# Attention before two expert layers on one core: the short tile's sums by GpSimd, the next batch's sums in parts, values read earlier

## The chip, the cores and the metric

The kernel runs on one core of a Trainium2 chip. Times are microseconds of device time for one execution; single stretches and instructions are given in the same unit, from the start of the profiled span.

## The reference

Attention over 4 batches, 8 heads, 576 tokens and 64 dimensions, in float32, with a bias from running sums, and then two layers of the kind x, activation, x on the 2304 tokens (512 to 2048 to 512).

```
scores = scale * q @ k^T                       # [4, 8, 576, 576], causal
cum    = cumsum(maximum(s, 0), -1)             # [4, 8, 576]
scores = scores + minimum(-(cum[:, None] - cum[None, :]), 0)
attn   = softmax(scores);  x = attn @ v        # [2304, 512] after joining the heads
h = x @ w_in;   x = (h * tanh(softplus(h))) @ w_out
h = x @ w2_in;  out = (h * sigmoid(1.702 h)) @ w2_out
```

The bias of a row is the same constant for every column except for the column's own running sum, so the kernel only adds the sum of the column and lets the row's extreme value take out the rest.

## The kernel before

**Tiling.** Per batch there are five tiles of query rows, four of 128 and a short one of 64 (576 = 4 x 128 + 64). The 8 heads come in two groups of 4. A group of one tile is worked off in steps: each step does the scores of one or several heads (`do_qk`, on TensorE), adds the running sums and takes the extreme value in one VectorE instruction (`do_max`, line 525, in the trace the custom instruction that reads `s` and `ck`), exponentials on ScalarE (`do_exp`), a split in two float16 parts (`do_hilo`, line 550), which are brought to the layout of the second product by a transposing DMA on SP (`pt<-hl`), and four steps later the product with v (`do_av`). In the short tile two heads share the 128 partitions: heads 0 and 1 of a group stand in partitions 0 to 63, heads 2 and 3 in 64 to 127. Batch 0 is done in another form that transposes on TensorE; there the running sums of its first two tiles come through a product.

**The running sums in SBUF.** They are computed once, written to DRAM (`cum_d`), and read back broadcast over the partitions. `load_ck` (line 372) allocates a tile of 128 x (4 heads x 512 columns) for one group, and loads it in two parts, columns 0 to 127 and 128 to 511. There is one buffer for each group (tag `ck0`, `ck1`). `load_ckp` (line 384) is for the short tile: it allocates a new tile in the same buffer, named `cp` in the trace, so that it waits for the last reader of `ck`, and loads 64 partitions x 2 heads x 576 columns twice, with DMAs on SP. The call stands after the last step of the fourth tile's group (line 695); the call for the next batch's sums stands after the last step of the short tile's group (line 697).

**The values' scale.** The split of v needs the largest value of the batch. `vscale_load` (line 310) reads all of a batch's v in three loads of 384 KB on SP into three rotating buffers (`vl`, of the five in pool `mo_a`, which the first layer's results `hs` use as well) and takes three maxima on VectorE (`vm`); `vscale_set` (line 321) makes the scale. `VSTEP` (line 639) says with which tile and group of the batch before they are queued: both with the short tile, group 0 and group 1. Steps of preparation are queued two groups ahead (`queue_prep(gi + 2)`, line 682), and popped over the steps of the group that runs, so the loads come out with the fourth tile's scores.

**Order.** The code is one emission order; a planner then orders each engine's instructions by readiness, with this order as priority. Each engine and DMA queue takes its instructions in order. SP issues the transposing DMAs, the sums, the values for the scale and the first layer's results `h_d`; GpSimd issues the loads of k, q and v (`kraw`, `qraw`, `vraw`), splits some weights and normalises x. The first layer's products (`h<-xh,w`) run on TensorE between the attention's from the first tiles on, up to about 410 us; the rest of the layers follows.

At the start some products without use keep TensorE busy while the first loads come (`warm`, line 813); they are the same in both kernels.

Of the kernel before, what the change touches and what calls it, by code (L numbers as in the profile page):

```python
# [9 lines left out]
F32 = mybir.dt.float32  # L10
# [79 lines left out]
def attention_moe_moe_kernel(  # L90
# [12 lines left out]
    nc = Line(tc.nc, lambda i, j: tc.add_manual_dep(i, j.name, order, reason="order of emission"))  # L103
    B, H, S, D = q.shape
# [6 lines left out]
    HG = H // 2  # L111
# [10 lines left out]
    cum_d = dram.tile([B, H, S], F32, name="cum_d")  # L122
# [18 lines left out]
    ck_p = enter(tc.tile_pool(name="ck", bufs=1))  # L141
# [36 lines left out]
    def held(d):  # L178
        if anchor[0] is not None and nxt[0] < NEAR:
            tc.add_manual_dep(d.ins, anchor[0].ins.name, order, reason="not before these scores")  # L180
        return d
# [153 lines left out]
    LK = S // 128 * 128  # L335
# [34 lines left out]
    ck, ckp = {}, {}  # L370

    def load_ck(b, g):
        t = ck_p.tile([128, HG * LK], F32, tag=f"ck{g}", name=f"ck{g}").rearrange("p (h t) -> p h t", t=LK)
        ck[b, g] = t
        load_ck_part(b, g, 0, 128)
        load_ck_part(b, g, 128, LK)

    def load_ck_part(b, g, c0, c1):
        held(nc.sync.dma_start(
            out=ck[b, g][:, :, c0:c1],  # L380
            in_=cum_d[b:b + 1, g * HG:(g + 1) * HG, c0:c1].to_broadcast([128, HG, c1 - c0]),
        ))

    def load_ckp(b, g):
        t = ck_p.tile([128, HG * LK], F32, tag=f"ck{g}", name=f"cp{g}")
        t = t[:, 0:HG // 2 * S].rearrange("p (h t) -> p h t", t=S)
        for a in range(2):
            h0 = g * HG + 2 * a
            nc.sync.dma_start(
                out=t[64 * a:64 * a + 64], in_=cum_d[b:b + 1, h0:h0 + 2, :].to_broadcast([64, 2, S])  # L390
            )
        ckp[b, g] = t

# [18 lines left out]
    last_of = {}  # L412
    for idx, x in enumerate(steps):
        gi = groups.index((x["b"], x["i"], x["g"]))
# [89 lines left out]
    def do_qk(x):  # L504
        b, i, g, n, L = x["b"], x["i"], x["g"], x["n"], x["L"]
        x["S"] = []
        for c0, c1 in segs(x):
            ps = ps_s.tile([128, 512], F32, tag="s", name="s")
            x["S"].append(ps)
            for e, hs in enumerate(x["hs"]):  # L510
                o = ps[:, e * L:e * L + c1 - c0]
                for a, h in enumerate(hs):
                    hl = h - g * HG
                    for w in range(2):
                        nc.tensor.matmul(
                            out=o, lhsT=qw[b, i, g][:, hl, w, :], rhs=kw[b, g][:, hl, c0:c1],
                            start=(e == a == w == 0), stop=False, skip_group_check=True,
                        )
                if c1 == L:
                    anchor[0] = nc.tensor.matmul(  # L520
                        out=o[:, c1 - c0 - n:c1 - c0], lhsT=identb, rhs=maskb if n == 128 else maskp,
                        start=False, stop=True, skip_group_check=True,
                    )

    def do_max(x):
        b, i, g, L = x["b"], x["i"], x["g"], x["L"]
        mx = sm_p.tile([128, HG], F32, tag="mx", name="mx")
        x["P"] = p = pp.tile([128, S], F32, tag="P", name="P", bufs=PB)
        for e, hs in enumerate(x["hs"]):
            hl = hs[0] - g * HG  # L530
            c = ckp[b, g][:, hl] if len(hs) == 2 else ck[b, g][:, hl]
            for f, (c0, c1) in enumerate(segs(x)):
                nc.vector.tensor_tensor_reduce(
                    out=p[:, e * L + c0:e * L + c1], in0=x["S"][f][:, e * L:e * L + c1 - c0], in1=c[:, c0:c1],
                    scale=1.0, scalar=mx[:, e:e + 1] if f else 3.0e38, op0=ALU.add, op1=ALU.min,
                    accum_out=mx[:, e:e + 1],
                )
        x["mx"] = mx

    def do_exp(x):  # L540
        ts = tile_state(x)
        L, p = x["L"], x["P"]
        for e in range(x["mu"]):
            o = p[:, e * L:(e + 1) * L]
            lut(
                o, o, AF.Exp, bias=x["mx"][:, e:e + 1], scale=-1.0,
                accum_out=ts["sums"][:, x["j"] + e, 0:1],
            )

    def do_hilo(x):  # L550
        L, mu, nb = x["L"], x["mu"], x["nb"]
        w = mu * L
        nblk = 2 * w // 128
        hl = pp.tile([128, 2 * NTIL * 128], F16, tag="hl", name="hl", bufs=HLB)
        p = x["P"]
        nc.scalar.activation(out=hl[:, 0:w], in_=p[:, 0:w], func=AF.Copy, scale=PSC)
        body = w // 128 * 128
        for c0, c1, o in ((0, body, 2 * w - body), (body, w, w)):
            if c0 < c1:
                nc.vector.scalar_tensor_tensor(  # L560
                    out=hl[:, o:o + c1 - c0], in0=p[:, c0:c1], scalar=PSC, in1=hl[:, c0:c1],
                    op0=ALU.mult, op1=ALU.subtract,
                )
        x["T"] = d = pt_p.tile([128, 2 * NTIL, 128], F16, tag="pt", name="pt")
        last_pt[0] = nc.sync.dma_start_transpose(out=d[:, 0:nblk, :], in_=hl[:, 0:2 * w])
# [70 lines left out]
    prep_q = []  # L636
    late_k = {}

    VSTEP = {(4, 0): vscale_load, (4, 1): vscale_set}

    NE = 4

    def queue_prep(gi):
        if gi >= len(groups):
            return
        b, i, g = groups[gi]
        items, vs, kT = split_items(b, i, g)
        if b == 0 and i == 2:
            for i_ in range(2):
                prep_q.append(lambda i_=i_: k_turn(0, i_, g, raw.pop((0, i_, g))))  # L650
        if NE < gi < len(groups) - 1:
            prep_q.append(lambda: load_group(*groups[gi + 1]))
        if i == 0 and b > 0:
            late_k[groups.index((b - 1, NTIL - 1, g))] = kT
        else:
            items = items + [kT]
        items = items + vs
        if b + 1 < B and (i, g) in VSTEP:
            items = items + [lambda: VSTEP[i, g](b + 1)]
        prep_q.extend(items)  # L660

    def pop_prep(m):
        for _ in range(min(m, len(prep_q))):
            prep_q.pop(0)()
# [8 lines left out]
    def tick():  # L673
        t = nxt[0]
        nxt[0] += 1
        if t < NS:
            x = steps[t]
            gi = x["gi"]
            if first_of[gi] == t:
                if gi > NE:  # L680
                    pop_prep(len(prep_q))
                queue_prep(gi + 2)
            if t >= NEAR:
                nc.mode = None
            left = last_of[gi] - t + 1
            npop = -(-len(prep_q) // left)
        else:
            npop = len(prep_q)
        if t < NS:
            do_qk(x)  # L690
            do_max(x)
            do_exp(x)
            if last_of[gi] == t and gi in late_k:
                late_k.pop(gi)()
            if last_of[gi] == t and x["i"] == LK // 128 - 1:
                load_ckp(x["b"], x["g"])
            if last_of[gi] == t and x["i"] == NTIL - 1 and x["b"] + 1 < B:
                load_ck(x["b"] + 1, x["g"])
            if x["b"]:
                do_hilo(x)  # L700
        pop_prep(npop)
        if 0 < t <= NS and steps[t - 1]["b"] == 0:
            early_pt(steps[t - 1])
        while avn[0] < NS and t - avn[0] >= lag(avn[0])[0]:
            x = steps[avn[0]]
            if x["b"]:
                do_av(x)
            else:
                early_av(x)
            if x["last"]:  # L710
                if x["b"]:
                    norm_tile(x)
                emit_q.append((t + lag(avn[0])[1], x))
            avn[0] += 1
        while emit_q and emit_q[0][0] <= t:
            emit_tile(emit_q.pop(0)[1])
# [110 lines left out]
    for t in q0:  # L827
# [4 lines left out]
        out=maskb, in_=maskb, pattern=[[-1, 128]], compare_op=ALU.is_ge, fill=BIG, base=0, channel_multiplier=1  # L832
# [62 lines left out]
    for a in range(2):  # L895
        nc.gpsimd.affine_select(
            out=maskp[64 * a:64 * a + 64], in_=maskp[64 * a:64 * a + 64], pattern=[[-1, 64]],
# [114 lines left out]
    while attn_left():  # L1012
        tick()
# [13 lines left out]
    for m in range(NF):  # L1027
        if m % 2 == 0:
            t = tmp_pair(F32, "hs")
        o = t[:, m % 2 * 512:m % 2 * 512 + 512]  # L1030
# [4 lines left out]
        if m % 2:  # L1035
            nc.sync.dma_start(
                out=h_d[:, m - 1:m + 1, (NU - UE) * U:NT], in_=t.rearrange("p (m t) -> p m t", m=2)
# [193 lines left out]
    for i, (u, t0, W, m0, n) in enumerate(groups1):  # L1231
# [10 lines left out]
        for j in range(n):  # L1242
# [3 lines left out]
            for c in range(KC):  # L1246
                a, o = divmod(c * W, 512)
# [125 lines left out]
    for u, (s0, W) in enumerate(spans):  # L1373
        for t0 in range(0, W, U):
            for jp in range(NP // 2):
# [10 lines left out]
                for e in range(2):  # L1386
                    o = slice(e * 512, (e + 1) * 512)
# [40 lines left out]
```

## Time and profile before

| what | us or share |
| --- | --- |
| median of 3 runs | 1015.3 (1012.83 to 1019.54) |
| profiled execution, its own time | 1021.99 |
| span in the profile | 1020.2 |
| TensorE busy | 973.8 |
| VectorE busy | 672.6 |
| ScalarE busy | 553.6 |
| GpSimd busy | 264.3 |
| mean granted clock | 0.99 |

The profile is that of one execution. All instructions that go through the kernel's recording helper have the same line (L76), so groups are read by the names of the tiles: `out<-in`.

### The profile page before, as it was taken

How to read it: one execution, taken by the hardware profiler on the slowest of the kernel's cores; microseconds unless marked ns; L12 is line 12 of the kernel's file. 1: busy time of each engine (PE TensorE's matmuls, PEld its weight loads, DVE VectorE, ACT ScalarE, POOL GpSimd, SP SyncE). 2: the span in 40 equal slices, each digit the busy share in tenths (PEclk: the TensorE clock that was granted, in tenths of full speed). 3: DMA queues.
4: the chain of work that ended last, by engine and by line, in shares of the span. 5: the costliest groups of instructions: out<-in, count | busy, mean ns of one | idle time of the engine just before them, and what ended most of it. 6: DMA issues, size and time to landing. Idle time of an engine off the chain costs nothing.

```text
span 1020.2 us, 20171 instructions
## 1 busy us (share of the span) xinstructions
PE 973.8 (95%) x7974; PEld 866.2 (85%) x7974; DVE 672.6 (66%) x1363; ACT 553.6 (54%) x1062; POOL 264.3 (26%) x318
## 2 busy tenths in 40 slices
PE   8889999968989999999999999999999999999997
PEld 7778988858979878998888888988888888888886
DVE  6679777754566787587998994994654653653553
ACT  4666677655646876486655663753433433433331
POOL 4634431233112410000000000054424434243341
PEclk9999999998999999999999999999999999999999
DMA  9932678996599969799997653400100100000000
GB/s 260 308 105 78 195 163 210 207 166 157 122 187 211 201 140 185 247 337 365 380 322 248 206 200 118 158 2 1 63 22 1 42 22 1 22 22 2 21 17 27
DMA packets 154863, 146.46 MB, mean 144 GB/s; under 512 B 89904, under 2 KB 123184, under 8 KB 154768
## 3 DMA queue, kind: packets, MB, share of 16 engines
q1 hardware_dynamic: 148352, 126.94, 45.4%
q0 software_dynamic: 6416, 18.23, 7.7%
q8 instruction: 63, 1.03, 0.4%
q14 instruction: 32, 0.26, 0.1%
HBM read 93.28 MB, written 32.58 MB: 123 GB/s over the span
## 4 chain that ended last, share of the span: by engine, by line
PE 81%; DMA 9%; DVE 5%; issue 2%; ACT 1%; POOL 1%; SPq 0%; DVEq 0%; POOLq 0%; ACTq 0%
PE h L76 29%; PE acc L76 24%; PE p L76 16%; DMA pt<-hl 5%; PE s L76 5%; PE o L76 3%; DMA kraw<-in_k_dram 2%; PE kt L76 1%; DVE wst L76 1%; PE qt L76 1%; PE pt L76 1%; PE xt L76 1%; DMA qraw<-in_q_dram 1%; POOL w L76 1%; DMA vl<-in_v_dram 0%
## 5 line engine op out<-in xcount | busy, mean ns | idle before, releaser
L76 PE MATMUL h<-x,w2i 128*128 128x256 f16 x1728 | 199.9, 273 | 0.9 <-DVE z L76 0.9
L76 PE MATMUL h<-xh,w 128*128 128x256 f32 x1344 | 193.4, 292 | 3.4 <-POOL w L76 3.2
L76 PEld LDWEIGHTS <-w2i 128*128 128x128 f16 x1728 | 169.0, 98 | 20.7 <-issue 1.1
L76 PE MATMUL acc<-gh,w 128*128 128x512 f32 (+1 forms) x640 | 181.7, 369 | 0.0
L76 PEld LDWEIGHTS h<-xh,w 128*128 128x128 f32 x1344 | 170.9, 193 | 6.0 <-POOL w L76 4.0
L76 PE MATMUL p<-w2l,gh 128*128 128x256 f16 x504 | 136.0, 273 | 0.0
L76 PE MATMUL p<-w2h,gl 128*128 128x256 f16 x504 | 135.9, 273 | 0.0
L76 PEld LDWEIGHTS acc<-gh,w 128*128 128x128 f32 x640 | 116.1, 189 | 20.6
L76 PE MATMUL p<-w2h,gh 128*128 128x256 f16 x504 | 133.3, 273 | 0.2 <-DVE e L76 0.2
L76 PE MATMUL acc<-gl,w 128*128 128x512 f32 (+1 forms) x320 | 117.9, 368 | 0.0
L76 DVE TENSOR_TENSOR gl<-z,gh 128x1024 fp32r<-128x1024 f32 (+1 forms) x72 | 94.5, 1313 | 27.9 <-ACT gh L76 27.0
L76 POOL TENSOR_TENSOR s<-z 128x256 f32<-128x256 f32 x72 | 56.4, 803 | 214.7 <-DVE z L76 214.7
L76 PEld LDWEIGHTS <-gh 128*128 128x128 f16 x1008 | 98.6, 98 | 11.7 <-issue 0.3
L76 ACT ACTIVATE sg<-h,spx 128x512 f32<-128x512 f32 x72 | 48.9, 680 | 109.7 <-PE h L76 109.7
L76 DVE SCALAR_TENSOR_TENSOR z<-h,sg 128x512 f32<-128x512 f32 x72 | 49.5, 688 | 71.5 <-ACT sg L76 71.5
L76 ACT ACTIVATE P<-P,mx 128x384 f32<-128x384 f32 (+4 forms) x128 | 76.3, 597 | 32.4 <-DVE mx L76 32.1
L76 DVE TENSOR_TENSOR gl<-s,gh 128x1024 f16<-128x1024 f32 x36 | 44.4, 1232 | 65.4 <-ACT gh L76 65.4
L76 ACT ACTIVATE gh<-z 128x1024 fp32r<-128x1024 f32 (+1 forms) x72 | 68.0, 948 | 29.5 <-DVE z L76 24.3
L76 ACT ACTIVATE gh<-s 128x1024 f16<-128x1024 f32 x36 | 38.0, 1057 | 82.6 <-POOL s L76 82.6
L76 PE MATMUL s<-kw,qw 128*128 128x288 f32 (+4 forms) x352 | 78.9, 336 | 1.3 <-DVE mx L76 1.2
L76 DVE CUSTOM_DVE_ANT_0 P<-s,ck 128x384 f32<-128x384 f32 (+3 forms) x112 | 54.3, 504 | 30.4 <-PE s L76 26.5
L76 PEld LDWEIGHTS acc<-gl,w 128*128 128x128 f32 x320 | 60.4, 189 | 10.1
(145 smaller groups left out, 1626.4 us busy)
## 6 DMA issues: line engine op xcount, KB each, us to landing
h_d<-hs SPq DMA_DIRECT2D x36, 512.0 KB, 4.5
hg<-h_d SPq DMA_DIRECT2D x36, 512.0 KB, 6.0
wst<-in_moe_w_in_dram SPq DMA_DIRECT2D x32, 512.0 KB, 7.5
wst<-in_moe_w_out_dram SPq DMA_DIRECT2D x32, 512.0 KB, 5.6
ck<-cum_d SPq DMA_DIRECT2D x8, 768.0 KB, 8.2
cp<-cum_d SPq DMA_DIRECT2D x16, 288.0 KB, 4.9
x_d<-x SPq DMA_DIRECT2D x18, 256.0 KB, 2.7
out_dram<-o SPq DMA_DIRECT2D x9, 512.0 KB, 2.8
```

The costliest lines, as they stand in the source:

```text
L76: r = f(*a, **kw)
```

## The change

Three edits. The short tile's sums are no longer loaded again: GpSimd moves three half tiles of 64 x 512 inside `ck` so that each half of the partitions has its two heads at column 0 and 1024, and two DMAs, now in GpSimd's queue, add only the last 64 columns. The sums of batches 1 to 3 come in three parts: columns 0 to 127 and 128 to 255 where both parts stood, and 256 to 511 behind the last step of the first tile of that group. The loads and maxima for the values' scale are queued with the third tile, group 0, and not with the short one; for batch 1 that is the group whose preparation is emitted in the opening, before the first layer starts.

```diff
@@ load_ck
-        load_ck_part(b, g, 128, LK)
+        load_ck_part(b, g, 128, 256 if b else LK)
@@ load_ckp
-        t = ck_p.tile([128, HG * LK], F32, tag=f"ck{g}", name=f"cp{g}")
-        t = t[:, 0:HG // 2 * S].rearrange("p (h t) -> p h t", t=S)
+        c = ck[b, g].rearrange("p h t -> p (h t)")
+        move = lambda p0, o, i_: nc.gpsimd.tensor_copy(c[p0:p0 + 64, o:o + LK], c[p0:p0 + 64, i_:i_ + LK])
+        move(0, 2 * LK, LK)
+        move(64, 0, 2 * LK)
+        move(64, 2 * LK, 3 * LK)
+        t = c.rearrange("p (r t) -> p r t", r=HG // 2)[:, :, 0:S]
         for a in range(2):
             h0 = g * HG + 2 * a
-            nc.sync.dma_start(
-                out=t[64 * a:64 * a + 64], in_=cum_d[b:b + 1, h0:h0 + 2, :].to_broadcast([64, 2, S])
+            nc.gpsimd.dma_start(
+                out=t[64 * a:64 * a + 64, :, LK:S], in_=cum_d[b:b + 1, h0:h0 + 2, LK:S].to_broadcast([64, 2, S - LK])
             )
         ckp[b, g] = t
@@ VSTEP
-    VSTEP = {(4, 0): vscale_load, (4, 1): vscale_set}
+    VSTEP = {(2, 0): vscale_load, (4, 1): vscale_set}
@@ tick
             if last_of[gi] == t and x["i"] == LK // 128 - 1:
                 load_ckp(x["b"], x["g"])
+            if last_of[gi] == t and x["i"] == 0 and x["b"]:
+                load_ck_part(x["b"], x["g"], 256, LK)
             if last_of[gi] == t and x["i"] == NTIL - 1 and x["b"] + 1 < B:
                 load_ck(x["b"] + 1, x["g"])
```

## Rows read from the trace of the kernel before

**Rows 1.** Busy time, share and count of each engine, whole span.

```profile
PE 973.8 (95%) x7974; PEld 866.2 (85%) x7974; DVE 672.6 (66%) x1363; ACT 553.6 (54%) x1062; POOL 264.3 (26%) x318
```

**Rows 2.** TensorE's waits: who for whom, us in total, times, longest.

```profile
PE o L76 <- DMA pt<-hl: 22.4, 14, 9.2
```

**Rows 3.** Busy time by stretches: length, engines, then clock, DMA share, GB/s.

```profile
61.00:70.00 9.00, 7.18 (x47) 6.19 (x48) 6.58 (x17) 6.42 (x17) 0.62 (x1) 0.81 0.11 33
145.00:165.00 20.00, 18.01 (x177) 15.87 (x176) 15.63 (x38) 15.30 (x41) 5.50 (x6) 1.00 0.78 140
190.00:220.00 30.00, 25.67 (x261) 22.85 (x259) 19.58 (x66) 19.33 (x54) 11.10 (x15) 1.00 1.14 192
220.00:240.00 20.00, 9.29 (x74) 8.69 (x73) 9.18 (x22) 9.68 (x27) 6.18 (x10) 0.74 0.98 162
300.00:311.00 11.00, 7.18 (x57) 6.21 (x56) 6.08 (x19) 4.79 (x13) 0.00 (x0) 0.84 1.03 190
345.00:370.00 25.00, 21.45 (x205) 19.32 (x204) 21.57 (x54) 20.94 (x58) 8.38 (x12) 1.00 0.92 168
```

**Rows 4.** DMA issues from 240 to 285 us: count, KB each, median landing.

```profile
kraw<-in_k_dram POOLq DMA_DIRECT2D x2, 128.0 KB, 3.5
pt<-hl SPq DMA_TRANSPOSE x10, 3.1
```

**Rows 5.** The same from 205 to 235 us.

```profile
kraw<-in_k_dram POOLq DMA_DIRECT2D x4, 128.0 KB, 8.8
...
pt<-hl SPq DMA_TRANSPOSE x5, 10.9
```

**Rows 6.** From 88 to 106 us: SP's queue (packets, MB, share) and issues.

```profile
q1 hardware_dynamic: 605, 1.47, 30.0%
...
cp<-cum_d SPq DMA_DIRECT2D x4, 288.0 KB, 5.3
h_d<-hs SPq DMA_DIRECT2D x1, 512.0 KB, 5.2
```

**Rows 7.** The chain that ended last, its DMAs: start, us, what.

```profile
55.53 5.50 DMA kraw<-in_k_dram
...
216.24 16.40 DMA pt<-hl
...
286.59 4.83 DMA vl<-in_v_dram
...
297.91 8.54 DMA pt<-hl
```

**Rows 8.** SP's issues in order of time: start, us, what.

```profile
170.64 0.66 SPq L76 DMA_DIRECT2D vl<-in_v_dram  x1
...
195.78 0.92 SPq L76 DMA_DIRECT2D ck<-cum_d  x2
...
206.42 1.14 SPq L76 DMA_DIRECT2D ck<-cum_d  x2
...
393.54 1.18 SPq L76 DMA_DIRECT2D cp<-cum_d  x2
```

**Rows 9.** The tile of the values' maxima: duration min/median/max ns, then waits.

```profile
L76 DVE TENSOR_REDUCE vm<-vl x9: 936/944/953, 81.1 to 296.3; 128x1 f32<-128x768 f32 x9
...
  DVE vm L76: 4.1, 2
```

**Rows 10.** GpSimd in order of time, with idle time before and what ended it.

```profile
365.07 0.64 POOL L76 DMA_DIRECT2D qraw<-in_q_dram  x1
384.04 1.35 POOL L76 TENSOR_TENSOR x<-x,rs 128x512 f32<-128x512 f32 x1 [18.32 <-DVE x L76]
```

**Rows 11.** VectorE in order of time: the maxima on the running sums.

```profile
138.12 0.42 DVE L76 CUSTOM_DVE_ANT_0 P<-s,ck 128x256 f32<-128x256 f32 x1
...
217.94 0.42 DVE L76 CUSTOM_DVE_ANT_0 P<-s,ck 128x256 f32<-128x256 f32 x1
...
392.72 0.69 DVE L76 CUSTOM_DVE_ANT_0 P<-s,ck 128x512 f32<-128x512 f32 x1
...
399.57 0.46 DVE L76 CUSTOM_DVE_ANT_0 P<-s,cp 128x288 f32<-128x288 f32 x1
```

## The prediction

> **What bounds the kernel now.** TensorE is busy 973.8 of 1020.2 us [rows 1], so a change elsewhere can only give back TensorE's idle time, or the time in which it runs at the lower clock. I first asked the table of waits what TensorE waits for: the largest entry is the transposing DMA that brings the exponentials to the layout of the second product, 22.4 us in 14 waits [rows 2]. Next come the stretches [rows 3]: the reader should compare PE's busy time with the length, and look at the clock beside it. From 190 to 220 us PE is idle 30.0 - 25.7 = 4.3 us, from 220 to 240 us 10.7 us, with a mean clock of 0.74; from 300 to 311 us 3.8 us at 0.84; from 345 to 370 us 3.6 us; from 145 to 165 us 2.0 us; from 61 to 70 us 1.8 us at 0.81. [...] At full clock, 220 to 240 us would have held (1 - 0.74) x 20 = 5.2 us more; part of that fell on idle time, so I count 3. In 300 to 311 us it is at most 1.8, in 61 to 70 us at most 1.7.
>
> These stretches lie at the turns from batch 1 to 2 and from 2 to 3. The chain of waits names what ended last in them: a transposing DMA issued at 216.24 us that lands 16.4 us later, the load of the values for the scale at 286.59 us (4.8 us) followed by a transposing DMA of 8.5 us, and at 55.53 us a load of k of 5.5 us [rows 7]. In the quiet stretch from 240 to 285 us the same transposing DMA lands after 3.1 us [rows 4], from 205 to 235 us after 10.9 us in the median [rows 5], while the share of the DMA engines is 1.14 from 190 to 220 us, against 0.78 from 145 to 165 us [rows 3]. So the bound at the turns is the DMA engines' backlog.
>
> **The change, part by part.** The rate of such loads: from 88 to 106 us SP's queue moved 1.47 MB in 30.0% of 18 us = 5.4 us, so 0.27 MB per us, most of it the short tile's sums [rows 6].
>
> *Short tile's sums on GpSimd.* Removed are 4 loads of 288 KB per batch, 1.18 MB or 4.3 us of all engines; added are 4 of 64 partitions x 2 x 64 floats = 32 KB, 0.13 MB or 0.5 us. Those 288 KB landed after 5.3 us where 512 KB to h_d took 5.2 [rows 6]. [...]
>
> SP loses 16 issues and with them a wait: the old load could only start when the last product's maximum had read the tile, and transposing DMAs stood behind it on SP. That wait moves to GpSimd, where the loads of k, q and v stand behind it. Per group GpSimd gets three copies of 64x512. The trace has no such copy; the 128x512 product with two operands takes 1.35 us [rows 10]; a copy reads one operand, so I set half of it as the lower end: 2.1 to 4.1 us for three; then two DMA issues of 0.64 us [rows 10]. GpSimd stands idle 18.3 us before one of its products [rows 10], so the work itself costs nothing while that idle time covers it. What counts is the serial chain. In the tightest group, the second of the last batch, the last maximum on the full sums ends at 392.72 + 0.69 = 393.4 us and the first on the short sums of that group stands at 399.57 us [rows 11], while the old loads were issued at 393.54 us [rows 8]. The new chain needs 2.1 to 4.1 + 1.3 + a landing of 3.5 (quiet) to 8.8 (full) [rows 4, 5] = 6.9 to 14.2 us against 6.2 of slack. The other groups mostly have a longer gap. I take 1 us in all, bounds 0 to 12.
>
> *Next batch's sums in more parts.* For batches 1 to 3 each group loads 256 + 256 KB first, and 512 KB when the first tile's scores are out. The bytes stay the same; 1 MB per batch moves behind the first tile. For batch 2 the loads stood at 195.78 and 206.42 us [rows 8] and the second tile starts at 217.94 us [rows 11], so both late parts are out before the transposing DMA of 216.24 us, or just behind it, and for that stop I give no credit. Only the third tile needs them. Cost and gain nothing, 6 more SP issues.
>
> *Values read at the third tile.* Three loads of 384 KB (1.18 MB, 4.3 us) and three VectorE passes of 0.94 us [rows 9] move two tiles forward, for all three batches that need a scale. So 4.3 us of transfers leave the turns (they stood at 170.64 [rows 8] and 286.59 us [rows 7]) and come back beside the second tile: for batch 1 about 138 us, for batch 2 about 218 to 224 us [rows 11], and for the first batch into the opening.
>
> **The sum.** *Turn 1 to 2:* from 170 us on, vl 4.3, short sums 4.3 and full sums 7.7 us were added, and the landing grew from 3.1 to 16.4 us, by 13.3. Without vl and most of the short sums 8.1 of these 16.3 go, so the DMA of 216.24 us lands 6.6 to 8.1 us earlier. Of 10.7 + 4.3 us idle and 3 us of slow clock I take 10.5 away. Against it stand the loads of batch 3's values at 218 to 224 us, 4.3 us into the same queue behind it: 3. Net -7.5, bounds 0 to -16. *Turn 2 to 3:* vl and two short loads leave the chain: -5, bounds 0 to -5.6. *345 to 370 us:* -1, bounds 0 to -3.6. *Opening:* vl no longer stands beside the load of k at 55.53 us, but its passes come earlier: -1, bounds -3.5 to +4.3. *138 to 165 us:* the new place of vl beside transposing DMAs that already stop PE for 2.0 us: +2.5, bounds 0 to 4.3 + 2.8 = 7.1. *GpSimd chain:* +1. What is late next is again a transposing DMA behind loads of k, q, v. Sum -11.0.
>
> The profiled execution took 1022.0 us (1020.2 span, 1.8 around it), 6.7 over the median 1015.3 of the runs; 1022.0 - 11.0 = 1011.0, so against the median **1004.3 us**.
>
> **Rivals.** *The stop only moves* (25%): the late parts of the sums and vl at 218 to 224 us refill the queue just where it ran over. For it: the DMA share is above 1 all through 190 to 220 us [rows 3], and all but 1.05 MB per batch still has to come through. Against it: less is in the queue on arrival. Turn 1 to 2 then gains 3 instead of 7.5 and loses some at 138 us: 1015.3 - 3 = 1012.
>
> *Slower, because VectorE is held by the value passes* (15%): VectorE takes its instructions in order, and a pass that stands early waits for a load that lands late; behind it stand the maxima, then the exponentials and the transposing DMAs. The waits for vl are 4.1 us already, in two places [rows 9]. At 218 to 224 us a load lands some 10.9 us after its issue [rows 5]. If it lands more than about one step (5 us) after VectorE reaches the pass, TensorE stops for some 10 us and restarts at the lower clock (3), the opening loses 4.3 and 138 us 4.3, less 5 + 5 of gain: +12, 1027 us. Against it: VectorE is itself idle about half of the time from 220 to 240 us [rows 3].
>
> *Slower sums through GpSimd* (8%): loads that GpSimd issues land after 3.5 us in quiet and 8.8 us in full stretches [rows 4, 5], and the slack of 6.2 us above is smaller than the upper end. Late by 3 us in four of eight groups: 12 - 11 = +1, 1016 us. [...]
>
> *The change doesn't act* (6%): the planner puts the moved steps back beside the old ones: 1015.
>
> **Chances.** The forecast has 46%, with its own range 997 to 1011. Faster by over 1% (a measurement of this kernel tells about that: the three runs spread from 1012.8 to 1019.5): 0.46 x 0.7 + 0.04 from the moved stop + 0.02 from the rest = 0.38. Slower by over 1%: 0.13 from held VectorE + 0.02 + 0.02 = 0.17. Within: 0.45. The range 994 to 1022 leaves out most of the case at 1027 and the bounds at which every gain comes in full, together under 2 in 10.
>
> **What would show it.** Right: the wait of PE for the transposing DMA falls from 22.4 to about 10 us; that DMA lands within 10 us at the turn to batch 2; no stop of over 4 us there; the clock stays above 0.9 in these stretches; SP shows no short-sum loads. The GpSimd chain is wrong if VectorE waits for the short sums. The step on the values is wrong if VectorE waits for vl for more than the old 4.1 us. What would make me wrong as a whole: if the backlog comes not from bytes but from transposing DMAs and the 256-byte rows of k, q, v getting in each other's way; then removing broadcasts does little.

## The result and the profile after

| kernel | runs | median us | lowest to highest |
| --- | --- | --- | --- |
| before | 6 | 1014.26 | 1011.99 to 1019.54 |
| changed | 6 | 1006.08 | 1003.62 to 1007.35 |

The ratio of changed to before is 0.9908, 95% interval 0.9879 to 0.9938: 8.2 us less by the medians. The profiled executions differ by more, 1022.0 against 1005.0 us, because that of before was 7 to 8 us over its median; a second one is among the experiments.

The page's line of busy time, which answers to [rows 1]:

```profile
PE 972.0 (97%) x7974; PEld 866.1 (86%) x7974; DVE 674.5 (67%) x1363; ACT 554.9 (55%) x1062; POOL 288.8 (29%) x358
```

TensorE does the same work; its idle time fell from 46.4 to 1002.9 - 972.0 = 30.9 us. The waits, first TensorE's [rows 2], then VectorE's [rows 9] (us in total, times, longest):

```profile
PE o L76 <- DMA pt<-hl: 1.6, 2, 1.1
...
DVE vm L76 <- DMA vl<-in_v_dram: 11.2, 3, 6.5
```

TensorE's wait for the transposing DMA is all but gone: 1.6 us, from 22.4. VectorE's wait for the values grew to 11.2 us, from 4.1. The stretches of [rows 3]:

```profile
61.00:70.00 9.00, 6.77 (x48) 5.18 (x47) 4.83 (x11) 4.91 (x13) 4.25 (x6) 1.00 0.27 76
145.00:165.00 20.00, 18.06 (x175) 16.55 (x174) 16.87 (x46) 17.84 (x49) 6.87 (x9) 1.00 0.86 185
190.00:220.00 30.00, 30.00 (x322) 28.09 (x320) 23.68 (x81) 24.00 (x65) 12.61 (x17) 1.00 1.04 217
220.00:240.00 20.00, 16.21 (x125) 14.84 (x121) 11.96 (x29) 11.52 (x32) 6.05 (x10) 0.83 0.94 236
300.00:311.00 11.00, 11.00 (x100) 10.66 (x99) 6.68 (x22) 6.24 (x14) 3.76 (x5) 1.00 0.96 174
345.00:370.00 25.00, 23.93 (x221) 20.76 (x221) 20.01 (x50) 19.44 (x48) 4.61 (x7) 1.00 0.66 140
```

The reader should look at PE's busy time first (25.67 of 30 and 9.29 of 20 us before at the turn to batch 2, now 30.00 and 16.21; 7.18 of 11 before at the next turn, now 11.00), and then at the last two columns: the share of the DMA engines is only a little smaller than before at the turn, 1.04 and 0.94 against 1.14 and 0.98, but the GB/s are higher, 217 and 236 against 192 and 162. Fewer bytes at the one rate by which the prediction priced them, 0.27 MB per us, would not show as a higher rate. The DMA view from 205 to 235 us [rows 5] says the same:

```profile
DMA packets 12970, 7.73 MB, mean 258 GB/s; under 512 B 9093, under 2 KB 12165, under 8 KB 12967
...
q0 software_dynamic: 645, 1.71, 20.7%
...
kraw<-in_k_dram POOLq DMA_DIRECT2D x4, 128.0 KB, 5.9
...
pt<-hl SPq DMA_TRANSPOSE x7, 5.1
```

and before, same stretch:

```profile
DMA packets 8968, 5.12 MB, mean 171 GB/s; under 512 B 6576, under 2 KB 8624, under 8 KB 8964
...
q0 software_dynamic: 516, 1.39, 40.9%
```

More bytes passed, 7.73 against 5.12 MB (the loads of the values stand here now, and the work comes earlier), yet the transposing DMA landed after 5.1 in place of 10.9 us. A packet of GpSimd's queue (the loads of k, q, v; packets, MB, share of 16 engines) took 0.409 x 30 us x 16 / 516 = 0.38 us before, 0.15 us now.

One place got worse, the opening. VectorE and SyncE (SP in the profile) there (start, us, what, idle before it):

```profile
50.76 2.88 DVE L76 TENSOR_REDUCE vm<-vl 128x1 f32<-128x768 f32 x3 [6.50 <-DMA vl<-in_v_dram]
```

```profile
36.90 3.56 SPq L76 DMA_DIRECT2D wst<-in_moe_w_in_dram  x1
40.51 4.09 SPq L76 DMA_DIRECT2D vl<-in_v_dram  x3
```

The first batch's pass now stands at 40.51 us right behind a weight load; VectorE waits 6.50 us for it with the rest of the opening queued behind.

### The profile page after: what moved, and what is told of

Its sections match the earlier page's. It is cut to its first block, busy times and chain, and to the rows that moved or that the text cites. A ratio compares the mean times of both kernels' runs of the same rounds, so it can differ in the third digit from the quotient of the medians.

```text
span 1002.9 us, 20218 instructions
## 1 busy us (share of the span) xinstructions
PE 972.0 (97%) x7974; PEld 866.1 (86%) x7974; DVE 674.5 (67%) x1363; ACT 554.9 (55%) x1062; POOL 288.8 (29%) x358
## 4 chain that ended last, share of the span: by engine, by line
PE 74%; DMA 4%; issue 2%; DVE 2%; ACT 2%; POOL 1%; SPq 0%; DVEq 0%; POOLq 0%; ACTq 0%
PE h L76 28%; PE acc L76 24%; PE p L76 16%; PE s L76 3%; PE o L76 2%; DMA qraw<-in_q_dram 2%; DMA pt<-hl 1%; DMA vl<-in_v_dram 1%; DMA vraw<-in_v_dram 1%; ACT P L76 1%; PE kt L76 0%; PE qt L76 0%; DVE w2l L76 0%; PE xt L76 0%; POOL vraw L76 0%
## 5 line engine op out<-in xcount | busy, mean ns | idle before, releaser
L76 PE MATMUL h<-xh,w 128*128 128x256 f32 x1344 | 197.2, 296 | 7.8 <-ACT w L76 3.0
L76 PEld LDWEIGHTS h<-xh,w 128*128 128x128 f32 x1344 | 173.8, 196 | 11.3 <-POOL w L76 3.9
L76 DVE CUSTOM_DVE_ANT_0 P<-s,ck 128x384 f32<-128x384 f32 (+4 forms) x128 | 61.5, 497 | 36.6 <-PE s L76 32.4
L76 POOL DMA_DIRECT2D x<-x_d x5 | 3.8, 766 | 237.3 <-DMA wst<-in_moe_w_in_dram 179.4
```

Of the source, the lines that this page charges most:

```text
L76: r = f(*a, **kw)
```

## The experiments

Idle us are a stretch's length less PE's busy time, one profiled execution each; MB and the median landing of the transposing DMA are from 205 to 235 us, at the turn to batch 2. The ratios are to the kernel before on the same chip. The medians come from several chips, on which the median of the kernel before was 1013.9 to 1016.7 us, so kernels are compared by the ratios.

| kernel | median us | ratio (95%) | idle 40-75 | 190-250 | 285-330 | 330-410 | MB | landing |
| --- | --- | --- | --- | --- | --- | --- | --- | --- |
| before | 1014.3 | 1 | 6.0 | 15.0 | 4.2 | 5.0 | 5.12 | 10.9 |
| before again | 1014.6, one run | | 5.1 | 11.6 | 3.6 | 5.1 | 5.34 | 9.6 |
| changed | 1006.1 | 0.9908 (0.9879 to 0.9938) | 8.0 | 3.8 | 0.4 | 2.3 | 7.73 | 5.1 |
| short sums alone | 1006.7 | 0.9925 (0.9901 to 0.9950) | 5.9 | 6.1 | 2.0 | 1.9 | 6.03 | 5.6 |
| parts alone | 1005.7 | 0.9908 (0.9873 to 0.9943) | 4.5 | 6.6 | 2.6 | 3.4 | 6.49 | 6.4 |
| values alone | 1016.8 | 1.0029 (1.0008 to 1.0049) | 7.6 | 11.6 | 2.2 | 5.1 | 6.34 | 9.5 |
| short sums and parts | 1003.6 | 0.9904 (0.9868 to 0.9939) | 5.7 | 4.9 | 0.6 | 2.2 | 5.82 | 6.9 |
| first values back | 1004.2 | 0.9912 (0.9884 to 0.9940) | 5.9 | 5.4 | 0.3 | 1.9 | 7.13 | 6.2 |
| values one tile earlier | 1002.5 | 0.9897 (0.9868 to 0.9927) | 5.5 | 2.5 | 0.9 | 2.4 | 6.60 | 5.9 |
| other queue | 1020.7 | 1.0070 (1.0032 to 1.0108) | 5.0 | 7.7 | 6.6 | 7.6 | 6.10 | 9.5 |
| bytes back, in DRAM | 1013.5 | 1.0005 (0.9978 to 1.0031) | 11.2 | 5.8 | 2.1 | 4.6 | 6.21 | 5.7 |
| bytes back, in place | 1006.2 | 0.9917 (0.9891 to 0.9943) | 6.4 | 4.2 | 1.8 | 3.9 | 5.94 | 6.6 |
| split, not moved | 1009.8 | 0.9938 (0.9910 to 0.9966) | 5.3 | 6.9 | 4.3 | 3.5 | 5.88 | 6.8 |
| parts, values one tile earlier | 1008.7 | 0.9938 (0.9908 to 0.9968) | 5.8 | 3.4 | 1.6 | 4.3 | 6.87 | 5.7 |

From 160 to 190 us, which the table leaves out, TensorE was idle 1.0 us in both traces of before, 0.7 in the changed kernel and 1.1 in short sums alone, but 3.3 in bytes back, in place, 3.2 in split, not moved, 3.2 in values one tile earlier, and 8.2 in other queue.

The expectations weigh three explanations. The bytes theory is the prediction's: TensorE stops because the DMA engines have too much to move at the turns. The SyncE theory: the load of the short sums waits for its buffer in SyncE's queue and holds the transposing DMAs behind it. The order theory: the planner's order came out differently by chance.

**Short sums alone.** The kernel before with the new `load_ckp` of the change and nothing else.

> Kernel before with one part of the change: the short tile's sums reordered on GpSimd, 64 columns loaded there; the two parts and the values' load as before. Bytes theory (the DMA engines' backlog at the turns is what the PE stops wait for, and it goes with the bytes removed): 4.3 us of transfer less at each turn, so the wait of PE for pt falls from 22.4 us to about 12 and the time to 1006 to 1010. SyncE theory (the waiting load of the short sums held the transposes behind it on its queue; bytes don't matter): all of the gain is here, 1004 to 1007, wait for pt under 5 us. Order theory (the list of work came out in another order by chance): no relation, 1008 to 1020 with the wait for pt still over 15 us.

Measured: 1006.7 us, ratio 0.9925, wait of PE for `pt` 6.6 us. The time fits both the bytes and the SyncE theory; the wait lies between the 12 of the one and the 5 of the other.

**Parts alone.**

```diff
-        load_ck_part(b, g, 128, LK)
+        load_ck_part(b, g, 128, 256 if b else LK)
...
+            if last_of[gi] == t and x["i"] == 0 and x["b"]:
+                load_ck_part(x["b"], x["g"], 256, LK)
```

> Kernel before with the second part alone: the next batch's sums for columns 256 to 512 are loaded one tile later, short sums and values as before. Bytes theory: 1.05 MB, 3.9 us of transfer, leave the crowded stretch of each turn and come back some 10 us later: wait of PE for pt from 22.4 to about 13 us, time 1007 to 1011. SyncE theory: no gain, because the short sums' load still stands in the queue: 1013 to 1017, wait for pt over 18 us. Order theory: anything from 1008 to 1020 with the wait for pt over 15 us.

Measured: 1005.7 us, wait 10.5 us. The SyncE theory in its form for the short sums falls: their load still stood in SyncE's queue. The prediction had given this part nothing. Short sums and parts bring 0.75% and 0.92% alone, 1.7% if they added up, and 0.96% together (below): most of what they take away is the same stop.

**Values alone.** `VSTEP = {(2, 0): vscale_load, ...}` in the kernel before.

> Kernel before with the third part alone: the pass over the next batch's values begins two tiles earlier. Bytes theory: 1.18 MB more, 4.3 us, into the turn 1 to 2, so its stop grows by about 3 us, and in the first batch VectorE waits for the values some 6 us where it had none before; 138 to 170 us gains 2 to 3 us: 1014 to 1020. If the values were a gain of their own (they leave the fifth tile, where the loads of the next batch begin), 1008 to 1012. Order theory: not told by the waits, VectorE's wait for vl as in the kernel before (4.1 us).

Measured: 1016.8 us, slower by 0.3% (0.1 to 0.5). VectorE's wait for the values and the turn to batch 2:

```profile
DVE vm L76 <- DMA vl<-in_v_dram: 13.8, 4, 6.2
```

```profile
190.00:250.00 60.00, 48.41 (x446) 44.22 (x446) 38.35 (x113) 37.93 (x102) 18.59 (x26) 0.91 0.98 196
```

The loss in the opening came as expected (idle 7.6 us). With 1.18 MB of values beside the turn (issued from 220.55 us) the idle time there did not grow: 11.6 us, as in the second trace of before. As a test of the bytes theory this is weak, because the same edit takes 1.18 MB away just ahead of the turn: in the kernel before the values were issued from 170.64 us on [rows 8], here between 100 and 160 us. At the turn to batch 3, where the values' load is gone too, 2.2 us idle are left of 4.2 and 3.6.

**Short sums and parts.** The changed kernel with `VSTEP = {(4, 0): vscale_load, ...}`.

> Changed kernel with the pass over the values put back to its old place: short sums and parts together. Bytes theory: both reliefs add up at the turns as far as there is a stop (some 17 us of stops), and the first batch's wait for the values is gone: 1000 to 1005, faster than the changed kernel by 2 to 5 us, wait of PE for pt under 5 us. If the values' move carried a part of the gain: 1007 to 1012, slower than the changed kernel. SyncE theory: the same time as the short sums alone, within 2 us.

Measured: 1003.6 us. The two reliefs do add up at the turn to batch 3, where each alone leaves 2.0 and 2.6 us idle and both 0.6. Against the changed kernel it is 2.5 us less by medians, but 0.9904 against 0.9908 by the ratios, with overlapping intervals: no difference is shown.

**First values back.** The changed kernel, the place chosen by batch:

```diff
-    VSTEP = {(2, 0): vscale_load, (4, 1): vscale_set}
+    VSTEP = {0: {(4, 0): vscale_load, (4, 1): vscale_set}}
+    VLATE = {(2, 0): vscale_load, (4, 1): vscale_set}
...
-        if b + 1 < B and (i, g) in VSTEP:
-            items = items + [lambda: VSTEP[i, g](b + 1)]
+        vstep = VSTEP.get(b, VLATE)
+        if b + 1 < B and (i, g) in vstep:
+            items = items + [lambda: vstep[i, g](b + 1)]
```

> Changed kernel with only the first batch's pass (for batch 1) put back to its old place; those for batches 2 and 3 stay two tiles earlier. If the loss lies in the opening (VectorE's wait of 6.5 us for vl at 50.8 us): 1002 to 1004, like the kernel with short sums and parts alone, TensorE at 40 to 65 us back to 20 us busy from 17.5. If the loss is the pass beside the turn 1 to 2: 1005 to 1007, as the changed kernel.

Measured: 1004.2 us, and the opening's idle time is back to 5.9 us from 8.0. By the trace the loss lies there; the times alone (intervals overlap) don't show it.

**Values one tile earlier.** As the last, with `VLATE = {(3, 0): ...}`.

> Changed kernel with the first batch's pass at its old place and the passes for batches 2 and 3 one tile earlier than the old place, so between the old place and the changed kernel's. Bytes theory: the loads of v stand at neither a turn nor the end of a batch: 1000 to 1003, no stop over 3 us at 214 to 235 us. If the values' place matters in the opening alone: within 1 us of the run that puts only the first pass back.

Measured: 1002.5 us, ratio 0.9897, the lowest of all; idle at 190 to 250 us 2.5 us. Its interval overlaps that of the changed kernel, so it is at least as good, no more.

**Other queue.** The kernel before, `load_ckp` with one word changed:

```diff
-            nc.sync.dma_start(
+            nc.gpsimd.dma_start(
                 out=t[64 * a:64 * a + 64], in_=cum_d[b:b + 1, h0:h0 + 2, :].to_broadcast([64, 2, S])
```

> Kernel before with the short tile's sums loaded whole, 288 KB each, from GpSimd's queue in place of SyncE's: the bytes and the wait for the buffer as before, no copies. Bytes theory: no gain beyond a microsecond or two, 1012 to 1017, wait of PE for pt 15 to 25 us. SyncE theory (the held load kept the transposes behind it): the gain of the short sums on GpSimd, 1004 to 1008, wait for pt under 8 us. GpSimd holding its own loads of k, q and v behind the wait would make it slower: 1018 to 1025.

Measured: 1020.7 us (its profiled execution was the slowest of the twelve, with a span of 1028.3). GpSimd's waits, us in total, times, longest:

```profile
POOL cp L76 <- DVE mx L76: 36.6, 3, 19.6
...
POOL cp L76 <- DVE vs L76: 27.3, 3, 12.8
```

The wait for the buffer holds GpSimd for up to 19.6 us, with the loads of k, q and v behind it; idle from 130 to 190 us rose from 2.0 to 8.3 us. In the changed kernel its waits for the copies' turn are 34.7 us in ten, 10.6 at the longest. So this run prices GpSimd as the place of a waiting load; a gain on SyncE, if there was one, is buried in it. Against one stands parts alone, where the load still waits on SyncE.

**Bytes back, in DRAM.** Short sums alone, and at each of its loads SyncE also copies 288 KB from `cum_d` to a DRAM buffer that nothing reads (this kernel does extra work, its output is unchanged).

```diff
+    spare = dram.tile([B * H // 2, 64, 2, S], F32, name="spare")
...
+            nc.sync.dma_start(
+                out=spare[b * H // 2 + h0 // 2], in_=cum_d[b:b + 1, h0:h0 + 2, :].to_broadcast([64, 2, S])
+            )
```

> Short sums alone on GpSimd (1006.7 us), and the bytes that this saves put back: at the same point SyncE also copies 288 KB of sums per pair of heads to a buffer in DRAM that nothing reads and that no instruction waits for. Bytes theory: the backlog is back, 1012 to 1017, wait of PE for pt back from 6.6 to over 14 us. SyncE theory (the wait for the buffer was the matter, and it is still gone) and order theory: 1005 to 1009, wait for pt under 9 us.

Measured: 1013.5 us, which looks like the bytes theory and isn't. SyncE in order of time, and the opening's busy time:

```profile
40.21 17.35 SPq L76 DMA_DIRECT2D spare<-cum_d  x16
```

```profile
40.00:75.00 35.00, 23.83 (x166) 20.51 (x167) 14.15 (x29) 18.11 (x42) 14.21 (x15) 0.90 0.90 293
```

The copies wait for nothing, and the planner put all 16 into the opening. The loss is there (11.2 us idle against 5.9); at the turns to batches 2 and 3 the gain stayed. It prices 4.7 MB in the opening at some 5 to 7 us and is no test of the bytes at the turns.

**Bytes back, in place.** The same question with a load that can't come early: its destination is the part of `ck` that the copies have just freed (448 columns, 224 KB per pair of heads, into columns that nobody reads). That is 88% of the 256 KB saved; the 229 KB and 90% of the expectation mix two units.

```diff
+            nc.sync.dma_start(
+                out=c.rearrange("p (r t) -> p r t", r=HG // 2)[64 * a:64 * a + 64, :, S:2 * LK],
+                in_=cum_d[b:b + 1, h0:h0 + 2, 0:2 * LK - S].to_broadcast([64, 2, 2 * LK - S]),
+            )
```

> Short sums alone on GpSimd (1006.7 us), with bytes put back where the saved ones lay: after the copies SyncE loads 229 KB per pair of heads into columns of the buffer that nobody reads, 90% of the 256 KB saved, so not before the point at which the kernel before loaded its short sums. Bytes theory: nearly all of the gain of the short sums goes, 1011 to 1016. SyncE theory (the wait for the buffer mattered, this load waits for the copies as that one did): the same, but only where the trace shows SyncE held at these loads with transposes behind. Order theory and a gain that was chance: 1004 to 1009.

Measured: 1006.2 us, all of the gain still there. The loads stand where the old ones stood: ahead of batch 2 SyncE issues them at 176.09, 178.95, 188.79 and 192.05 us, the kernel before its own at 176.47, 178.41 and 188.39 (two). The DMA view from 175 to 205 us shows the bytes back ahead of the turn, 7.00 MB where short sums alone has 5.83 and the first trace of before 6.78:

```profile
DMA packets 12728, 7.00 MB, mean 233 GB/s; under 512 B 9697, under 2 KB 12257, under 8 KB 12724
...
ck<-cum_d SPq DMA_DIRECT2D x4, 224.0 KB, 5.5
```

The same from 205 to 235 us, and what TensorE waited for there:

```profile
DMA packets 10485, 5.94 MB, mean 198 GB/s; under 512 B 7970, under 2 KB 10018, under 8 KB 10482
...
q0 software_dynamic: 739, 1.90, 31.3%
```

```profile
222.18 0.52 PE L76 MATMUL o<-v,pt 128*128 128x128 f16 x8 [2.22 <-DMA pt<-hl]
...
225.05 0.82 PE L76 MATMUL o<-v,pt 128*128 128x128 f16 x8 [1.24 <-DMA pt<-hl]
```

From 160 to 250 us TensorE is idle 7.5 us, against 7.2 in short sums alone and 16.0 and 12.6 in the two traces of before. The bytes theory of the short sums falls here, and with it the SyncE theory: a load that waits for the buffer stands in SyncE's queue again, at the old times, and the gain stays.

**Split, not moved.** The kernel before, with the full sums in three pieces at the old point.

```diff
-        load_ck_part(b, g, 128, LK)
+        load_ck_part(b, g, 128, 256 if b else LK)
+        if b:
+            load_ck_part(b, g, 256, LK)
```

> Kernel before with the next batch's sums loaded in three pieces in place of two, all at the old point: the two parts without their later date. Bytes theory in the strict form (only what lies in the crowded stretch counts): no gain, 1012 to 1016, wait of PE for pt over 15 us. If smaller transfers, or the first columns landing sooner, were what helped: 1004 to 1008. Order theory: anything between.

Measured: 1009.8 us, 0.9938. No byte leaves the turn. TensorE's busy time there, this kernel and then the first trace of before:

```profile
160.00:190.00 30.00, 26.77 (x243) 23.19 (x244) 21.42 (x54) 20.02 (x49) 4.09 (x5) 1.00 1.04 210
190.00:250.00 60.00, 53.07 (x503) 49.36 (x502) 36.23 (x112) 39.70 (x106) 21.02 (x29) 0.94 0.99 192
```

```profile
160.00:190.00 30.00, 29.04 (x263) 25.35 (x261) 22.90 (x61) 21.89 (x55) 4.09 (x5) 1.00 1.01 213
190.00:250.00 60.00, 44.96 (x421) 41.30 (x419) 33.04 (x100) 34.92 (x94) 19.98 (x27) 0.91 0.97 172
```

Of 15.0 and 11.6 us idle from 190 to 250 us only 6.9 are left, but 3.2 stand ahead of it; from 160 to 250 us it is 10.2 us, against 16.0 and 12.6. At the turn to batch 3 nothing is gained (4.3 us idle, 4.2 and 3.6 before).

**Before again.**

> The kernel before unchanged, a second profiled execution. Its first one took 1022.0 us where the median is 1014 to 1015. If the long stop of that trace (one wait of 9.2 us for pt at the turn 1 to 2) is in every execution: again over 8 us idle in one piece there. If it was the bad end of a spread: several stops of 1 to 4 us, TensorE at 190 to 250 us busy 49 to 53 us in place of 45.0, and a time of 1012 to 1016.

Measured: 1014.6 us. TensorE at the turn to batch 2, this execution and then the first (start, us, what, idle before it):

```profile
228.36 0.82 PE L76 MATMUL o<-v,pt 128*128 128x128 f16 x8 [8.33 <-DMA pt<-hl]
```

```profile
232.68 0.82 PE L76 MATMUL o<-v,pt 128*128 128x128 f16 x8 [9.25 <-DMA pt<-hl]
```

The long stop is in both, at the same instruction, and 190 to 250 us are 48.4 us busy against 45.0. So the stop belongs to the kernel before, and 3.5 us of its idle time in the first trace to that execution alone.

**Parts, values one tile earlier.** "Values one tile earlier" with the old `load_ckp`.

> The best kernel so far (both sums parts, first values at the old place, the others one tile earlier: 1002.5 us) with the short sums loaded whole by SyncE as in the kernel before. Bytes theory with one stop that either relief takes away: 1003 to 1007, up to 4 us slower than with the copies on GpSimd. If the copies on GpSimd cost as much as their bytes bring once the parts are there: 1001 to 1003. If both reliefs count in full: 1010 or more.

Measured: 1008.7 us (1003.5 to 1011.1), 0.9938. It fits one stop that either relief takes away, and the short sums leave some gain beside it; the intervals don't settle how much.

## Why the time came out, and the reason didn't

The time was 1006.1 us for a forecast of 1004.3 (8.2 us less than before by the medians, forecast 11.0), and the gain lay where the forecast had it. Its reason failed, so that the time came out is in good part luck: the terms for the turns were priced by bytes, which the runs do not bear out, the part priced at nothing brings 0.9% alone, and the misses elsewhere cancel (the opening came out 3 to 4 us worse than forecast, 138 to 165 us and GpSimd's chain together 3.5 us better). Of its signs of being right, the wait for the transposing DMA fell further than forecast (1.6 us for about 10), and the clock from 220 to 240 us, 0.83, stayed below the 0.9 it named. By steps:

**Turn 1 to 2, forecast -7.5.** Idle time at 190 to 250 us fell from 15.0 and 11.6 to 3.8 us, so the size was about right. The step "So the bound at the turns is the DMA engines' backlog", priced at a fixed 0.27 MB per us, is the one that failed. With 88% of the short sums' bytes back in place the gain stays; a split that moves nothing makes the kernel 0.6% faster, and of 16.0 and 12.6 us idle from 160 to 250 us it leaves 10.2. The credit for the values isn't borne out here either: moved alone, they leave the stop as in the second trace of before. The rival of a stop that only moves did not come: the late parts of the sums and the values did go in at 212.76 to 217.5 us, and TensorE's longest wait for `pt` is 1.1 us. What goes with the stop is how long the transfers take: in the three traces with over 11 us idle there (before twice, values alone) the transposing DMA landed after 9.5 to 10.9 us in the median, as it did in other queue, whose stops are spread over more places; in the ten others after 5.1 to 6.9. The bytes moved in these 30 us do not tell them apart: 5.82 to 7.73 MB in the ten, 5.12 and 5.34 in the kernel before, but 6.34 in values alone and 6.10 in other queue; and where the stop is shorter, more of the work falls into the stretch. A DMA share of 0.98 to 1.15 went with 171 to 258 GB/s in these fourteen traces, so the share does not say how many bytes stand in line.

**Why the packets are slow** in the kernel before stays open. The prediction named the candidate that would make it wrong: transposing DMAs and the rows of k, q, v in each other's way. The price of a packet of GpSimd's queue, 0.38 and 0.30 us in the two traces of before, 0.27 and 0.26 in values alone and other queue, 0.15 to 0.25 in the ten others, is in line with that, though the highest of the ten (0.25, short sums and parts) lies next to the 0.26, and a long packet may go with the stop without being its cause. Nothing was run that changes these loads alone, so the cause is not shown. Three other explanations have the traces against them. The order of TensorE's work: around 219 us the changed kernel has the same sequence of scores, second products and first-layer products as before but for one group of transposes, only with `pt` there in time. The order of SyncE's queue: behind the last load of the full sums, both traces of before, bytes in place and split issue the same, one transposing DMA, `h_d`, two transposing DMAs, `h_d`, transposing DMAs. And full sums that land too late: VectorE waits for them 1.7 to 2.5 us in the three traces with the long stop and in other queue, and 0 to 3.6 us in the ten others.

**Next batch's parts, "cost and gain nothing".** Wrong: alone they bring 0.9% (0.6 to 1.3). The credit was refused because the moved bytes would be out before the transposing DMA anyway; that is the same bytes argument. Some or all of it can be the split itself, which brings 0.6% (0.3 to 0.9) without any move; the intervals do not settle what the move adds.

**Turn 2 to 3, forecast -5.** 285 to 330 us: 4.2 and 3.6 idle before, 0.4 now, about -3.5. Each sums part alone gives about half, and so do the values alone (2.2 left); both sums parts give nearly all, a split without the move gives none, as the forecast would have it; but with the short sums' bytes back in place it stays at 1.8. So for the short sums the bytes don't carry this turn either.

**Opening, forecast -1 (-3.5 to +4.3).** Wrong in sign: idle at 40 to 75 us rose from 6.0 and 5.1 to 8.0. This is the rival of held VectorE in one of its three places: it had priced the opening at 4.3 us; the wait was 6.5 us and the price 2 to 3 us. By the prediction's own test (VectorE waits for the values more than the old 4.1 us; 11.2 now) the step on the values is wrong, and values alone is slower by 0.3%. At 218 to 224 us, where the rival had its 10 us, VectorE waits 2.0 us for them, and TensorE is idle 3.8 us in all of 190 to 250 us.

**138 to 165 us, forecast +2.5.** Nothing: 145 to 165 us has 18.06 us busy, 18.01 before [rows 3]; the loads stood at 122.75 us, earlier than I had put them, and VectorE waited 2.7 us for them without a stop of TensorE behind it.

**GpSimd chain, forecast +1 (0 to 12).** No cost seen: TensorE and VectorE wait nowhere for the short sums, and short sums alone is as fast as parts alone. The copies (duration ns min/median/max) took 0.61 us each in the median, below the lower end of 0.7 us:

```profile
L76 POOL COPY ck<-ck x24: 601/610/1129, 83.2 to 375.5; 64x512 f32<-64x512 f32 x24
```

Why the longest copy took 1.13 us, no run tells.

**345 to 370 us, forecast -1.** 3.6 and 3.4 us idle in the two traces of before, 1.1 now: -2.4, within the bounds.

## What to carry to other kernels

In these traces a DMA share near 1 was no measure of a backlog in bytes (0.98 to 1.15 went with 171 to 258 GB/s): read the GB/s and the time per packet beside it, in the same stretch, before pricing a stop by bytes. To test a bytes argument, put the bytes back where they were, with a dependence that pins them (the free copies of bytes back, in DRAM, were all issued from 40.21 us on, in the opening, and spoiled the test), and profile the kernel before twice. A pass that waits for a load is moved only to where the load has long landed, batch by batch; here the opening was not such a place (a wait of 6.50 us).

## What the runs showed of the hardware

The same 16 engines, at a share of 1.1 of their time, moved 171 GB/s in the kernel before, 216 in parts alone and 258 in the changed kernel from 205 to 235 us, with the same kinds of transfers, but not the same number of each (five transposing DMAs against eight and seven); the transposing DMA landed after 3.1 us in quiet [rows 4] and 16.4 at worst [rows 7]. Splitting each 768 KB broadcast of batches 1 to 3 into 256 and 512 KB at the same point was worth 0.6% (0.3 to 0.9) of the whole kernel, while the bytes stay the same and SyncE has six issues more; why is not shown.
